# Rows of the fp16 value tiles 96 elements apart in place of 66

## The chip, the cores and the metric

The kernel runs on one core of a Trainium2 chip. Its engines have their own instruction streams: TensorE (PE in the profile, with PEld for its weight loads), VectorE (DVE), ScalarE (ACT), GpSimd (POOL) and SyncE (SP), which issues most of the transfers. The metric is the device time of one launch in microseconds. Before the change the median of three runs was 413.39 us (412.63 to 414.4).

## The reference

Cosine attention over 8 batches and 12 heads (448 positions, 64 features), then a mixer over tokens and channels. Everything arrives and leaves as float32.

```python
q_n = q / (norm(q) + 1e-6);  k_n = k / (norm(k) + 1e-6)
attn = softmax(q_n @ k_n.T / tau)                 # 448 x 448 per head, tau = 0.1
x = concat_heads(attn @ v)                        # (8, 448, 768)
h = relu(x.T @ w_tok1) @ w_tok2                   # 448 -> 256 -> 448 over tokens
u = x + h.T
out = u + relu(u @ w_ch1) @ w_ch2                 # 768 -> 1536 -> 768 over channels
```

## The kernel before

The unit of attention is a pair of heads of one batch: 8 batches x 6 pairs = 48 pairs. The 448 positions are cut into 4 chunks (NCH) of 112, one position of each chunk per partition. For pair i, `load` brings q, k and v to tiles ql, kl and vl, five pairs ahead. `squares`, `norm_sum`, `norm_root` and `norm_rec` make the inverse norms on GpSimd, VectorE and ScalarE; `normalize` writes the normed q and k in fp16 (tile qkn); `tpose_pe` (TensorE and a copy, in the first pairs) or `tpose_dma` (a transposing transfer) turns them (tile qkT). `score` (line 257) computes k times q per chunk of keys into PSUM tile pS, and `expo` (line 264) takes the exponential on ScalarE into tile pE in fp16.

The values take their own way. `v_cast` (line 214) casts vl, eight runs of 64 floats per partition (2 heads x 4 chunks), into one of four fp16 tiles v16s, used in turn by pair number. VectorE does 39 of these casts through `recast` (line 128) and ScalarE nine (line 220). A v16 tile has eight rows, one per head and chunk, each EV elements long: 64 values, a one in element 64, and the rest unused. The ones are written once, at the start (line 103), and give the sum of the exponentials as a 65th output column.

`pv` (line 267) then multiplies: for a block of 128 query positions and head h, four matmuls over the chunks c accumulate into one 65-column slice of PSUM tile pO. The 128 columns of pE are the stationary operand, and the 65 elements of row 4h + c of the value tile are the moving one. c = 0 starts the group (it overwrites) and c = 3 ends it:

```python
nc.tensor.matmul(pO[:, n, h, :], s["p"][:, c, h, c0:c0 + 128],
                 s["v16"][:, NCH * h + c, 0:E + 1],
                 start=(c == 0), stop=(c == NCH - 1))
```

Three blocks of positions are done in one call (24 matmuls), the fourth in another (8), so a pair has 32 and the kernel 1536. VectorE then takes the reciprocal of column 64 (line 284) and multiplies (line 285) into x16.

The mixer of a batch is a list of jobs: tokens up and down (`tok1` line 309, `tok2` line 322 and 327, in batch 0 their pairwise forms on lines 347 and 358), the residual add (line 331), a cast and a transposing transfer of u into uT (line 338), then channels up (`ch1`, line 375) and down (`ch2`, line 384), each with an evacuation by ScalarE (line 377) or VectorE (line 388), and the store.

The order on every engine is written out by hand. Pairs 0 to 12 run through `opening`, the others through `slot`, and `fill` puts mixer jobs between their steps by a credit of estimated matmul time. So mixer work of earlier batches fills TensorE between the attention steps of later ones, and after the last pair only mixer work remains.

The tiles of pool cst are laid out one after another: the identity, then the four value tiles, then all the rest, and the other pools behind them. The first value tile begins at byte 16768 of each partition, a multiple of 64.

Of the kernel before, what the change touches and what calls it, by code (L numbers as in the profile page):

```python
# [23 lines left out]
def kernel(  # L24
# [21 lines left out]
    B, H, S, E = q.shape  # L46
# [7 lines left out]
    NDH = D // DH  # L54
    NPAIR = H // 2
    NG = B // 2
    EV = E + 2
    inv_tau = 1.0 / float(tau)
    EPS_NORM = 1e-6

# [23 lines left out]
    id16 = cst.tile([128, 128], FP16, name="id16")  # L84
    v16s = [cst.tile([P, 2 * NCH, EV], FP16, name=f"v16_{n}") for n in range(4)]
    nns = [cst.tile([P, 2, 2 * NCH, 2], FP32, name=f"nn_{n}") for n in range(3)]
# [525 lines left out]
```

## Time and profile before

| what | value |
|---|---|
| median of three runs | 413.39 us |
| the profiled execution | 413.88 us |
| its span, first to last instruction | 411.5 us |
| PE busy | 383.9 us, 93% |
| ACT busy | 262.1 us, 64% |
| DVE busy | 233.9 us, 57% |
| POOL busy | 198.2 us, 48% |
| line 278, value matmuls | 1536, 64.8 us busy, 196 ns mean |
| line 128 on v, VectorE casts | 39, 24.9 us |
| granted TensorE clock, mean | 0.992 |

Busy time of one group is the union of its instructions. TensorE's matmuls overlap in the pipeline: one of line 278 is shown as 196 ns, but the next starts some 30 ns after it. The time that matters for such a row is therefore the distance between starts. The chain of waits is the work that ended last, followed back from the last instruction; a group's share of it is the time that the end depended on it in this execution.

### The profile page before, as it was taken

The page shows a single profiled execution, that of the slowest core. Times are in us where ns is not written, and L with a number is a line of the kernel's source. Part 1 is how long each engine was busy: PE and PEld are TensorE (multiplying, and loading weights), DVE is VectorE, ACT ScalarE, POOL GpSimd, SP SyncE. Part 2 cuts the span into 40 slices and gives each one's busy share as a digit, 9 for nine tenths or more (in the row PEclk, how much of TensorE's full clock was granted, in tenths as well). Part 3 has the DMA queues.
Part 4 walks back from the last instruction along what each step waited for, and adds up shares of the span by engine and source line. Part 5 has one row for each costly group of instructions (what it writes and reads, how often), then busy time and mean ns, then how long its engine had stood idle before and what let it go on. Part 6 is the DMA issues. An engine that isn't in the chain of part 4 may idle for free.

```text
span 411.5 us, 9002 instructions
## 1 busy us (share of the span) xinstructions
PE 383.9 (93%) x3592; PEld 220.6 (54%) x3592; DVE 233.9 (57%) x530; ACT 262.1 (64%) x452; POOL 198.2 (48%) x207
## 2 busy tenths in 40 slices
PE   2768789899999999999999999999999999999996
PEld 1456556556445556555545556555545556655453
DVE  4499978748634776548643676448643683152022
ACT  6879869876576666765677666775677665522400
POOL 4979969934743564634653464635563430000000
PEclk9989989999999999999999999999999999999999
DMA  8899999966974588649876488539963253027013
GB/s 212 239 247 216 221 252 234 248 139 140 238 155 109 139 181 198 160 75 184 219 178 150 124 196 198 151 84 199 209 166 91 61 120 101 2 43 149 0 43 112
DMA packets 97385, 63.63 MB, mean 155 GB/s; under 512 B 57536, under 2 KB 93888, under 8 KB 97344
## 3 DMA queue, kind: packets, MB, share of 16 engines
q1 hardware_dynamic: 94032, 58.20, 60.1%
q0 software_dynamic: 3184, 4.72, 6.7%
q8 instruction: 28, 0.46, 0.5%
q10 hardware_dynamic: 128, 0.15, 0.1%
q14 instruction: 13, 0.11, 0.1%
HBM read 43.45 MB, written 11.01 MB: 132 GB/s over the span
## 4 chain that ended last, share of the span: by engine, by line
PE 78%; DVE 11%; DMA 3%; ACT 3%; POOL 2%; issue 1%; DVEq 0%; POOLq 0%
PE pG L375 27%; PE pF L384 25%; PE pO L278 9%; PE pS L257 9%; PE pR L309 5%; PE pU L322 3%; DVE ssq L187 2%; DVE x L285 2%; ACT pE L264 2%; DMA uT<-u 1%; DVE qkT L246 1%; DMA kl<-in_k_dram 1%; POOL qkn L211 1%; DVE u L366 1%; DVE u L331 1%; POOL sq L177 1%
## 5 line engine op out<-in xcount | busy, mean ns | idle before, releaser
L264 ACT ACTIVATE pE<-pS 112x896 f16<-112x896 f32 x192 | 164.9, 914 | 39.5 <-PE pS L257 38.8
L375 PE MATMUL pG<-uT,wc1t 128*128 128x384 f16 (+1 forms) x576 | 121.4, 355 | 0.3 <-DMA uT<-u 0.3
L384 PE MATMUL pF<-wc2t,gT 128*128 128x384 f16 x672 | 116.6, 326 | 0.2
L211 POOL TENSOR_TENSOR qkn<-ql,rn 112x512 f16<-112x512 f32 x48 | 50.1, 1044 | 137.7 <-DVE rn L199 122.4
L384 PEld LDWEIGHTS <-gT 128*128 128x128 f16 x672 | 63.6, 98 | 47.0 <-issue 7.3
L377 ACT ACTIVATE gT<-pG 128x384 f16<-128x384 f32 (+1 forms) x96 | 52.6, 548 | 45.9 <-PE pG L375 45.1
L375 PEld LDWEIGHTS <-wc1t 128*128 128x128 f16 x576 | 51.7, 98 | 51.9 <-issue 11.5
L388 DVE TENSOR_TENSOR u<-pF,u 128x384 f32<-128x384 f32 x56 | 31.1, 556 | 78.5 <-PE pF L384 78.0
L257 PE MATMUL pS<-qkT 64*112 64x448 f16 x384 | 60.2, 384 | 13.2 <-DVE qkT L246 10.3
L278 PEld LDWEIGHTS <-pE 112*128 112x128 f16 x1536 | 60.8, 100 | 15.9 <-issue 5.4
L278 PE MATMUL pO<-v,pE 112*128 112x65 f16 x1536 | 64.8, 196 | 0.0
L187 DVE TENSOR_REDUCE ssq<-sq 112x16 f32<-112x1024 f32 (+1 forms) x49 | 58.3, 1192 | 5.5 <-ACT sq L175 3.7
L284 DVE RECIPROCAL rec<-pO 128x6 f32<-128x6 f32 x96 | 17.5, 182 | 77.1 <-PE pO L278 76.1
L211 POOL TENSOR_TENSOR qkn<-kl,rn 112x512 f16<-112x512 f32 (+1 forms) x48 | 49.8, 1038 | 0.0
L177 POOL TENSOR_TENSOR sq<-ql 112x512 f32<-112x512 f32 x46 | 48.8, 1061 | 1.6 <-ACT qkT L244 1.2
L177 POOL TENSOR_TENSOR sq<-kl 112x512 f32<-112x512 f32 x46 | 48.5, 1053 | 0.2 <-DMA kl<-in_k_dram 0.2
L285 DVE TENSOR_TENSOR x<-pO,rec 128x384 f16<-128x384 f32 x96 | 40.9, 426 | 3.3
L257 PEld LDWEIGHTS <-qkT 64*112 64x112 f16 x384 | 19.0, 127 | 39.1 <-issue 22.8
L128 DVE TENSOR_REDUCE v<-vl 112x512 f16<-112x512 f32 x39 | 24.9, 639 | 3.4 <-DMA vl<-in_v_dram 3.4
L331 DVE TENSOR_TENSOR u<-pU,x 128x384 f32<-128x384 f32 x50 | 25.4, 545 | 0.1
L337 ACT CAST u<-u 128x768 f16<-128x768 f32 x14 | 11.6, 832 | 20.9 <-DVE u L331 20.9
L191 ACT ACTIVATE ln<-ssq 112x16 f32<-112x16 f32 (+1 forms) x49 | 10.9, 223 | 17.7 <-DVE ssq L187 17.5
(41 smaller groups left out, 181.9 us busy)
## 6 DMA issues: line engine op xcount, KB each, us to landing
ql<-in_q_dram SPq DMA_DIRECT2D x48, 224.0 KB, 3.8
kl<-in_k_dram SPq DMA_DIRECT2D x48, 224.0 KB, 4.0
vl<-in_v_dram SPq DMA_DIRECT2D x48, 224.0 KB, 4.2
out_dram<-u SPq DMA_DIRECT2D x8, 336.0 KB, 3.5
wc1t<-in_moe_w_ch_dram POOLq DMA_DIRECT2D x4, 576.0 KB, 7.5
wc2t<-in_moe_w_ch_dram POOLq DMA_DIRECT2D x3, 768.0 KB, 10.3
out_dram<-u SPq DMA_DIRECT2D x8, 288.0 KB, 3.8
out_dram<-u SPq DMA_DIRECT2D x7, 240.0 KB, 3.1
```

The lines of the kernel that those rows point to most:

```text
L177: nc.gpsimd.tensor_mul(out=s["sq"][:, j], in0=a, in1=a)
L187: nc.vector.tensor_reduce(out=small(i, "ssq")[:, j], in_=st_[i]["sq"][:, j], axis=AXX.X, op=ALU.add)
L211: eng.tensor_tensor(out=o, in0=s[nm][:, g], in1=_bcast_free(rn, E), op=ALU.mult)
L257: nc.tensor.matmul(pS[:, h, 0:S], s["T"][64 * h:64 * h + 64, 1, c * P:(c + 1) * P], s["T"][64 * h:64 * h + 64, 0, :], start=True, stop=True)
L264: nc.scalar.activation(out=s["p"][:, c], in_=s["pS"][c][:, :, 0:S], func=AF.Exp, scale=inv_tau)
L278: nc.tensor.matmul(pO[:, n, h, :], s["p"][:, c, h, c0:c0 + 128], s["v16"][:, NCH * h + c, 0:E + 1], start=(c == 0), stop=(c == NCH - 1))
L285: nc.vector.tensor_tensor(out=xt[hp:hp + nr, t0:t0 + len(ts), d0:d0 + 2 * E].rearrange("p t (h e) -> p t h e", h=2), in0=pO[m0:128, :, :, ...
L331: nc.vector.tensor_tensor(out=u32[:, i - t0, cols], in0=pU[:], in1=xt[:, i, cols], op=ALU.add)
L375: nc.tensor.matmul(pG[:], wc1t[:, dt, ct * 128:(ct + 1) * 128], uT[:, dt, :], start=(dt == 0), stop=(dt == DT - 1))
L377: nc.scalar.activation(out=gT[:, ct, :], in_=pG[:], func=AF.Relu)
L384: nc.tensor.matmul(pF[:], gT[:, ct, (i - t0) * 128:(i - t0 + 1) * 128], wc2t[:, ct, dh * DH:(dh + 1) * DH], start=(ct == 0), stop=(ct == C ...
L388: nc.vector.tensor_tensor(out=o, in0=pF[:], in1=o, op=ALU.add)
```

## The change

Only the number of elements from one row of a value tile to the next changes. E is 64.

```diff
-    EV = E + 2
+    EV = 3 * E // 2
```

Rows were 66 fp16 elements, 132 bytes, apart, and a tile 1056 bytes. They are 96 elements, 192 bytes, apart, and a tile is 1536 bytes. In the tile at byte 16768, rows began at 0, 4, 8, 12, 16, 20, 24 and 28 bytes past a multiple of 64; now all begin at such a multiple. The second and fourth tile began 32 past a multiple of 64, and now begin at one. What is read and written of a row, 65 elements, stays the same, and so do all instructions and their order. Every tile allocated behind the value tiles moves up by 4 x 480 = 1920 bytes.

## The prediction

> **What bounds the kernel now.** I read the page of the slowest (only) core first, parts 1, 4 and 5, then the chain of waits in order of time, then the waits of TensorE, then the busy time by stretches, and last the value matmuls of line 278 one by one. Part 1 and part 4 of the page:
>
> ```profile
> PE 383.9 (93%) x3592; PEld 220.6 (54%) x3592; DVE 233.9 (57%) x530; ACT 262.1 (64%) x452; POOL 198.2 (48%) x207
> ...
> PE 78%; DVE 11%; DMA 3%; ACT 3%; POOL 2%; issue 1%; DVEq 0%; POOLq 0%
> PE pG L375 27%; PE pF L384 25%; PE pO L278 9%; PE pS L257 9%; PE pR L309 5%; PE pU L322 3%; DVE ssq L187 2%; DVE x L285 2%; ACT pE L264 2%; DMA uT<-u 1%; DVE qkT L246 1%; DMA kl<-in_k_dram 1%; POOL qkn L211 1%; DVE u L366 1%; DVE u L331 1%; POOL sq L177 1%
> ```
>
> TensorE sets the end for 78% of the span, and the one instruction whose input the change moves, line 278 (value rows streamed against exp columns), stands in the chain by itself. Ordering the chain by time gives its share with one more digit: 9.5%, or 0.095 x 411.5 = 39.1 us. That share is not spread evenly. The busy time of each engine by stretches shows three stages (columns: stretch, its length, busy time and instructions of PE, PEld, DVE, ACT, POOL, granted clock, DMA share, GB/s):
>
> ```profile
> 0.00:103.00 103.00, 81.39 (x967) 51.43 (x968) 75.21 (x172) 80.96 (x142) 75.69 (x88) 0.97 0.95 215
> 103.00:376.30 273.30, 271.33 (x2460) 152.93 (x2459) 153.63 (x350) 174.00 (x298) 122.52 (x120) 1.00 0.63 145
> 376.30:411.50 35.20, 31.18 (x169) 16.26 (x166) 5.02 (x9) 7.17 (x12) 0.00 (x0) 1.00 0.21 57
> ```
>
> From 103 to 376 us PE is busy 271.33 of 273.30 us and no other engine over 174; after 376 us there is no line 278 at all. Before 103 us PE shares the bound. The waits of PE from 57 us to the end confirm that it hardly waits:
>
> ```profile
> PE pS L257 <- DVE qkT L246: 1.7, 3, 1.0
> PE pU L322 <- DVE x L285: 1.2, 2, 0.6
> PE pG L375 <- DMA uT<-u: 0.3, 1, 0.3
> PE pS L257 <- ACT pE L264: 0.2, 1, 0.2
> ```
>
> Next, line 278 and the casts that write the value rows (what writes or reads tile v; ns min/median/max):
>
> ```profile
> L278 PE MATMUL pO<-v,pE x1536: 191/193/262, 15.5 to 358.0; 112*128 112x65 f16 x192
> L128 DVE TENSOR_REDUCE v<-vl x39: 627/628/686, 19.6 to 344.5; 112x512 f16<-112x512 f32 x39
> L220 ACT CAST v<-vl x9: 601/603/620, 11.3 to 282.9; 112x512 f16<-112x512 f32 x9
> L103 POOL MEMSET v<- x4: 133/135/137, 1.3 to 1.4; 112x8 f16 x4
> ```
>
> The 191 to 193 ns are a pipelined latency; what PE pays is the distance between starts. One block at full clock, in windows that all begin at 60.00 us and end just past one start, so that the bracket counts the matmuls begun by then:
>
> ```profile
> 60.00:60.17 0.17, 0.14 (x5) 1.00 1.07 265
> 60.00:60.20 0.20, 0.17 (x6) 1.00 1.05 257
> 60.00:60.30 0.30, 0.27 (x9) 1.00 1.04 266
> 60.00:60.33 0.33, 0.30 (x10) 1.00 1.07 276
> 60.00:60.42 0.42, 0.40 (x13) 1.00 1.07 282
> 60.00:60.45 0.45, 0.42 (x14) 1.00 1.04 278
> ```
>
> Matmuls 5, 9 and 13 each open a group of four (chunk c = 0); from one of them to the next matmul it is 0.03 us, and from there three matmuls take 0.10 and 0.09 us. Over every such start at full clock in the trace, the c = 0 matmul holds PE for 29.15 ns on average (29 or 30, never more; the first matmul after another line, 35.5 on average, is left out), and the c = 1, 2, 3 matmuls for 32.89, 32.49 and 32.50, together 32.64. This is the observation on which the forecast stands. The row of v read is 4h + c and starts 132 x (4h + c) bytes into the tile, so rows 0 and 4 start at a multiple of 16 bytes, and the other six 4, 8 or 12 bytes past one. Tiles 1 and 3 start 32 bytes off a multiple of 64, and row 4 lies 16 off; these read at 29 too. So a multiple of 64 is more than is needed; a multiple of 16 would do.
>
> **The change, part by part.** No instruction is added, removed or reordered, on any queue; the row pitch goes from 132 to 192 bytes.
>
> (1) *Value matmuls.* 24 of the 32 per pair start off a 16-byte boundary. If the boundary is the reason for the longer hold, each goes from 32.64 to 29.15, 3.49 ns less, 24 x 3.49 = 84 ns per pair, 48 x 84 = 4.0 us in all. By stage: 103 to 376 us holds 1056 of the 1536 matmuls, 33 pairs, 2.8 us, all on the path because PE has no slack there. From 57 to 103 us there are 230, 7.2 pairs, 0.6 us, of which I take two thirds, 0.4, since PE is not alone in the chain there. Before 57 us (8 pairs, 0.6 us) the chain runs through VectorE from pair to pair (qkT, u, ssq, rec, x follow each other without a gap), and two of those pairs run at granted clock 0.50, where the four chunks hold PE for 54, 54, 55 and 57 ns, so hardly anything is to be had: 0. Sum 3.2 us. The chain gives the same: 39.1 us of it on line 278, times 84 / 1017 (the 32 matmuls of a pair are 8 x 29.15 + 24 x 32.64 = 1017 ns), is 3.2. Bounds: 0 and 4.0.
>
> (2) *What is late next.* A block of 24 on the chain takes 0.77 us (24 x 32) and would take 0.70. Its reader, the reciprocal of line 284, waits for it already (76.1 us of idle ahead of it, 43 times), so it starts earlier with it. Nothing that PE waits on stands near in the long stretch: 1.2 us for x, 0.3 for the transposed u, and both are downstream of PE. At 102.41 us the chain passes through one 5.73 us transposing transfer, whose own ancestors are ssq, the residual add and a PE block at 96.63; a gain made before 98 us therefore goes through it.
>
> (3) *The casts.* They write eight runs of 64 elements, now at aligned starts. VectorE's 628 ns for 512 elements is below what its contiguous cast of the same kind makes of it (line 128 on w1s, 809 ns for 640, or 647 for 512), so there is no penalty to remove; bounds from that row are 0 to +19 ns each, 39 x 19 = 0.7 us of VectorE time, and v is not among the groups of the chain's shares. ScalarE's 603 lies between nothing and the same 19 ns, 9 times. The four memsets (135 ns) lie at 1.3 us, under the first loads. Taken as 0; the cover is VectorE's 120 us of idle in the long stretch.
>
> (4) *Everything behind v in memory moves up by 1920 bytes*, 15 x 128: the loads' tiles go from 128 past a multiple of 256 to a multiple of 256, and u, u32, uT and x from 64 to 192 past one. No row compares such places directly. The nearest: ql, kl and vl have the same shape and land in 3.8, 4.0 and 4.2 us, so 0.2 us either way for one transfer; the chain holds one load each of ql (2.78) and kl (5.38) and one transpose of u (5.73), hence -0.6 to +0.6. I take 0.
>
> Sum: 3.2 us, against the profiled execution's 413.88 (span 411.5 and 2.4 around it): 410.7. That execution is 0.49 above the median of the three runs, 413.39; from the median it is 410.2.
>
> [...]
>
> **The rivals.** (A) *The group's first matmul is short because it is first, not because of its row.* In this kernel c = 0 is both the aligned row and the one that overwrites instead of accumulating; the two can't be told apart by which rows are short. Against it: in the groups of 12 on line 384 the first and the later matmuls are alike (162 to 164 ns medians), in the pairs of line 358 too (55.5 and 55.0), and at half clock the three accumulating chunks differ among themselves (54, 55, 57) in the order of their byte offsets 4, 8, 12. For it: none of those other groups has a moving operand this short. If so, nothing changes: 413.4, with part (4) 412.8 to 414.0.
>
> (B) *The gain is real but eaten before the end,* by PE reaching a transfer or VectorE sooner. For it: 102.41, where PE's wait for uT is 0.3 us and any gain that does not go through the chain is lost. Against it: only 3.4 us of PE waits after 57 us. Losing everything before 103 us and a quarter of the rest leaves 2.1 us: 411.3.
>
> (C) *The other side: the transposing transfers of u become slower, since u16 and uT move from 64 to 192 past a multiple of 256.* Place: uT<-u, 31 issues of 3.7 us median, ahead of each batch's line 375. The one at 102.41 has no slack. It decides from the point where that 5.73 has grown by the 3.2 us gained elsewhere, 56%. If all double, it costs 5.7 us there, and the six later batches cost from nothing to 3.7 us each, as their slack allows; PE shows no wait for them now, so I take 0.3 each, 1.8: 410.2 + 5.7 + 1.8 = 417.7. Against it: the qkT transposes, from yet another start (128), land in 3.0 us and those of u, a seventh larger, in 3.7, which leaves little for the start to have done.
>
> **How the numbers follow.** Forecast (rows' start, 3.2 us, between 2.4 and 4.6 with part 4): 0.72, 408.8 to 411.0. (B) 0.08, 411.0 to 411.6. (A) 0.12, 412.8 to 414.0. (C) 0.08, 414 to 418. A measurement tells about 0.5%, 2.07 us, from no change: faster is at or below 411.32. The forecast lies below it nearly whole (0.72, less 0.02 for noise), (B) half: 0.74. Slower, above 415.46: most of (C), 0.07. The rest, 0.19, is the same. The range leaves out (C) and a little beyond each end: 408.6 to 414.0.
>
> **What would show it.** Right: line 278's medians go to 191 ns for all; blocks of 24 on the chain take 0.70 to 0.71 us in place of 0.77; the stretch that holds 1056 of them is 2.8 us shorter; lines 375 and 384 keep their means (355 and 326). If blocks stay at 0.77, (A) holds. If they shrink and the span doesn't, look at PE's waits for uT and x (B). If landings of uT exceed 3.7 us, (C). The prediction is wrong above all if c = 0 is short for being first.

## The result and the profile after

The changed kernel takes 410.84 us (median of 12 runs, 409.57 to 413.12) against 413.34 for the kernel before (12 runs, the three made first among them). The ratio is 0.9933, 95% interval 0.9913 to 0.9953; the two medians by themselves give 0.9940. The forecast was 410.2 in 408.6 to 414.0: right sign, and 2.5 us gained where 3.2 were forecast. The reason given for it turned out wrong, as the experiments show.

Parts 1 and 4 of the page after the change:

```profile
PE 380.6 (93%) x3592; PEld 217.7 (53%) x3592; DVE 233.7 (57%) x530; ACT 261.5 (64%) x452; POOL 197.9 (49%) x207
...
PE 80%; DVE 12%; DMA 3%; SPq 2%; ACT 1%; issue 1%; DVEq 0%
```

TensorE (PE) is still the bound, and busy 3.3 us less; the other engines' busy times are the same within 0.6. What writes and reads the value tiles (ns min/median/max):

```profile
L278 PE MATMUL pO<-v,pE x1536: 191/193/247, 15.6 to 353.7; 112*128 112x65 f16 x192
L128 DVE TENSOR_REDUCE v<-vl x39: 627/628/687, 19.0 to 340.2; 112x512 f16<-112x512 f32 x39
L220 ACT CAST v<-vl x9: 601/603/621, 11.7 to 279.1; 112x512 f16<-112x512 f32 x9
```

The casts did not change (627/628/687 ns against 627/628/686), and neither did the 191/193 ns that a value matmul is shown with, of which 191 for all had been expected. The change is in the spacing, which shows in the blocks of 24 on the chain in order of time (start us, length us). After, and then before:

```profile
104.27 0.73 PE pO L278 x24
111.67 0.73 PE pO L278 x24
120.36 0.73 PE pO L278 x24
127.77 0.73 PE pO L278 x24
```

```profile
114.50 0.76 PE pO L278 x24
123.24 0.77 PE pO L278 x24
130.70 0.77 PE pO L278 x24
```

0.73 instead of the forecast 0.70. One by one at full clock, from the start of a matmul to the next start, the four chunks c = 0 to 3 now hold PE for 30.17, 30.64, 30.11 and 30.14 ns (before 29.15, 32.89, 32.49, 32.50). The slow three became faster and c = 0 became slower. The starts show how: about four matmuls follow at 29 or 30 ns and then one at 35, over and over, whichever chunk it is.

Where the time went is read by taking the start of the same matmul, by its number (counted from 0), in both traces. Both issue their 3592 matmuls in the same order.

| matmul | before, us | after, us | ahead by |
|---|---|---|---|
| 100th | 24.99 | 24.37 | 0.62 |
| 400th | 47.71 | 47.10 | 0.61 |
| 500th | 58.37 | 56.16 | 2.21 |
| 1000th | 106.92 | 104.47 | 2.45 |
| 3300th | 357.49 | 353.17 | 4.32 |

The first 0.62 us are no effect of the rows: the 100th matmul starts anywhere from 23.35 to 24.99 us in the kernels of this document, and the earliest of them has the slow rows. Between the 1000th and the 3300th lies the long stretch bound by PE, before and then after (the columns are those of the stretches in the prediction):

```profile
106.92:357.49 250.57, 248.60 (x2306) 139.50 (x2303) 143.89 (x329) 167.62 (x288) 118.60 (x117) 1.00 0.64 149
```

```profile
104.47:353.17 248.70, 246.92 (x2306) 137.88 (x2303) 143.90 (x329) 167.29 (x288) 118.50 (x117) 1.00 0.62 150
```

It is 1.87 us shorter, and by line (start to next start) 1.66 of it is line 278, 35.07 to 33.41. Another 0.33 is line 257, 33.42 to 33.09, which takes anything from 33.05 to 33.71 in kernels with either spacing and is scatter. The 1.6 us between the 400th and the 500th matmul are not the rows' doing: in this execution before, PE's granted clock was 0.50 in 53.3 to 56.7 us, and in this execution after it was 1.00 there, while it was half from 52 or 53 us on in three of the experiments whose rows are as fast (e1, e2, e5). So the two profiled spans differ by 4.3 us and the medians by 2.5.

What PE waits for after 57 us is, after the change (before: 1.7, 1.2 and 0.2, and 0.3 for uT):

```profile
PE pS L257 <- DVE qkT L246: 1.8, 3, 1.1
PE pU L322 <- DVE x L285: 1.3, 2, 0.7
PE pS L257 <- ACT pE L264: 0.2, 1, 0.2
```

### The profile page after: what moved, and what is told of

It is laid out like the page before. It is cut to its first block, busy times and chain, and to the rows that moved or that the text cites. A ratio compares the mean times of both kernels' runs of the same rounds, so it can differ in the third digit from the quotient of the medians.

```text
span 407.2 us, 9002 instructions
## 1 busy us (share of the span) xinstructions
PE 380.6 (93%) x3592; PEld 217.7 (53%) x3592; DVE 233.7 (57%) x530; ACT 261.5 (64%) x452; POOL 197.9 (49%) x207
## 4 chain that ended last, share of the span: by engine, by line
PE 80%; DVE 12%; DMA 3%; SPq 2%; ACT 1%; issue 1%; DVEq 0%
PE pG L375 27%; PE pF L384 26%; PE pO L278 9%; PE pS L257 9%; PE pR L309 5%; PE pU L322 3%; DVE ssq L187 2%; DVE x L285 2%; DMA ql<-in_q_dram 2%; DVE qkT L246 2%; DVE u L366 1%; DMA vl<-in_v_dram 1%; SPq L164 1%; DVE u L331 1%; DVE v L128 1%
## 5 line engine op out<-in xcount | busy, mean ns | idle before, releaser
L388 DVE TENSOR_TENSOR u<-pF,u 128x384 f32<-128x384 f32 x56 | 31.1, 555 | 77.9 <-PE pF L384 77.6
L278 PEld LDWEIGHTS <-pE 112*128 112x128 f16 x1536 | 58.2, 99 | 15.7 <-issue 5.1
L278 PE MATMUL pO<-v,pE 112*128 112x65 f16 x1536 | 62.1, 195 | 0.0
```

The costliest lines, as they stand in the source:

```text
L388: nc.vector.tensor_tensor(out=o, in0=pF[:], in1=o, op=ALU.add)
```

## The experiments

The theory first held was the prediction's: a row is read slowly if it does not start at a multiple of 16 bytes. Rivals were its rival (A), that the first matmul of a group is short, and that the place of the other tiles brought the gain.

**e1: a multiple of 16 bytes, not of 64.**

```diff
-    EV = E + 2
+    EV = E + 8
```

> Rows 72 elements (144 bytes) apart, so that each starts at a multiple of 16 bytes but mostly not of 64. If a start at a multiple of 16 bytes is what counts: line 278 keeps the spacing of the changed kernel (29 ns, every fifth 35; 30.3 on average), blocks of 24 take 0.73 us, and the time is that of the changed kernel, 410.8 (ratio to before 0.993). If 64 bytes are needed: rows at 16, 32 and 48 past a multiple hold PE for 32.6 ns again, and the time is 413.3 (ratio 1.000).

410.95 us, ratio 0.9940 [0.9912, 0.9968]; chunks 30.15, 30.73, 30.07, 30.14, blocks of 24 in 0.73 us. A multiple of 64 is not needed.

**e2: rows 96 apart, but all starting 4 bytes past a multiple of 64.** The rest lies where the changed kernel has it. The lines are set against the kernel before, as in all experiments but e9.

```diff
-    EV = E + 2
+    EV, VO = 3 * E // 2, 2
...
-            nc.gpsimd.memset(t[:, :, E:E + 1], 1.0)
+            nc.gpsimd.memset(t[:, :, VO + E:VO + E + 1], 1.0)
...
-        o = s["v16"][:, :, 0:E]
+        o = s["v16"][:, :, VO:VO + E]
...
-                                     s["v16"][:, NCH * h + c, 0:E + 1],
+                                     s["v16"][:, NCH * h + c, VO:VO + E + 1],
```

> Rows 96 apart as in the changed kernel, all tiles at the same addresses, but the 65 elements of each row moved up by two, so that every row, that of c = 0 too, starts 4 bytes past a multiple of 64. If the row's start is the cause: all four chunks hold PE for 32.5 to 33 ns, c = 0 no longer 29; 32 x (32.8 - 30.3) = 80 ns per pair above the changed kernel, 3.8 us in all, some 3.1 on the path: 413.9 (ratio 1.001, a little above before, whose c = 0 rows were aligned). If c = 0 is short because it opens the group: c = 0 stays at 29 and the time is 413.3. If the move of the tiles behind brought the gain: 410.8.

410.98 us, ratio 0.9934 [0.9910, 0.9958]; chunks 29.54, 31.15, 29.74, 29.19, 29.9 on average. Blocks on its chain:

```profile
105.54 0.72 PE pO L278 x24
112.93 0.72 PE pO L278 x24
121.61 0.72 PE pO L278 x24
```

Rows that all start 4 bytes past a 16-byte boundary are as fast as aligned ones. The theory on which the forecast stood falls here.

**e3: only the other tiles moved,** by an unused tile behind the value tiles; rows 66 apart.

```diff
-    nns = [cst.tile([P, 2, 2 * NCH, 2], FP32, name=f"nn_{n}") for n in range(3)]
+    pad = cst.tile([P, 960], FP16, name="pad"); nns = [cst.tile([P, 2, 2 * NCH, 2], FP32, name=f"nn_{n}") for n in range(3)]
```

> Rows 66 apart as before, and an unused tile of 1920 bytes behind the four value tiles, so that everything else lies where the changed kernel has it. If the gain is all the rows': 413.3, spacing 29 / 32.9 / 32.5 / 32.5 as before (ratio 1.000). If the new place of the load tiles brings part of it: 412.7 (0.9985) and an earlier start of the first value matmuls by up to 0.6 us; all of it: 410.8 (0.993).

413.43 us, ratio 0.9983 [0.9962, 1.0003]; chunks 29.15, 32.93, 32.49, 32.48, and the long stretch 250.20. Two of its blocks on the chain:

```profile
105.03 0.76 PE pO L278 x24
112.48 0.77 PE pO L278 x24
```

The place of the other tiles does nothing to the spacing. Its half-clock matmuls are worth a look: 57, 54, 54 and 55 ns for the four chunks, over and over, where the prediction had read 54, 54, 55 and 57 in the order of the byte offsets. The rows are the same, so that order does not belong to the offsets. Four of them take 220 ns in the kernel before, in e3 and in e1, whose rows are fast at full clock: in these traces the slow rows cost nothing at half clock.

**e4: streams of matmuls alone,** 96 of each form with a new stationary each, rows 128 elements apart; nothing else is computed. One line of it, wrapped here, 65 columns 4 bytes past a multiple of 64 (`mv(n, off, cols)` takes row n % 8 of a fp16 tile from byte `off` on, `st(n)` one of twelve stationary operands):

```python
for n in range(96): nc.tensor.matmul(ps[n // 4 % 3][0:128, 65 * (n // 12 % 2):65 * (n // 12 % 2) + 65],
                                     st(n), mv(n, 4, 65), start=(n % 4 == 0), stop=(n % 4 == 3))
```

> Leaves out the whole computation: it runs streams of 96 matmuls on TensorE, one form per line, and stores zeros and a few sums. 65 columns, groups of four, a new stationary for each. Row start theory: 0, 16 and 32 bytes past a multiple of 64 give 30.3 ns per matmul (2.9 us for 96), 2 to 14 bytes give 32.6 to 33 (3.1 us), with or without accumulation. Group opening theory: the start makes no difference, and the stream in which every matmul opens its own group is short at 12 bytes past too (2.8 us). [...]

Each window below runs from the first start of a stream to the first start of the next, so its length (second column) over 96 is the spacing. The other columns are PE's busy time, the matmuls in flight in the window, the clock, DMA share and GB/s. In order: 65 columns at 0, 4 and 12 bytes, 65 at 12 bytes with every matmul opening its own group; then, at 0 bytes, 57, 62, 64, 66 and 80 columns.

```profile
23.34:26.25 2.92, 2.92 (x97) 1.00 0.02 6
29.20:32.08 2.88, 2.88 (x102) 1.00 0.00 0
40.80:43.70 2.90, 2.90 (x102) 1.00 0.00 0
52.48:55.38 2.90, 2.90 (x102) 1.00 0.00 0
66.01:68.57 2.56, 2.56 (x103) 1.00 0.03 6
68.57:71.28 2.72, 2.72 (x103) 1.00 0.02 6
71.28:74.08 2.80, 2.80 (x102) 1.00 0.00 0
74.08:77.00 2.92, 2.92 (x102) 1.00 0.02 6
86.26:89.70 3.44, 3.44 (x101) 1.00 0.00 0
```

The start (30.0 to 30.8 ns over ten offsets) and the group's opening (2.90 us for 96 at 12 bytes either way) hardly count. At this pitch no stream of 65 columns averages the 31.8 of before, so neither theory explains it, and what is left is the pitch of 66 itself. The widths bear on the 35 ns of every fifth matmul. The averages are 26.67 ns for 57 columns, 28.33 for 62, 29.16 for 64, 30.30 for 65, 30.31 for 66, 31.67 for 70, 33.64 for 73 and 35.83 for 80. From 64 to 80 that is 0.417 ns a column, (35.83 - 29.16) / 16. With this slope the averages of 62, 64, 70 and 80 all lie 2.5 ns above columns times 0.417. Those of 65, 66 and 73 do not: they lie near 72, 72 and 80 times 0.417 (30.0, 30.0, 33.4), and that of 57 at 64 times (26.7), the width rounded up to a multiple of 8. The larger of the two, an estimate read off these eight averages, fits them within 0.35 ns. No stream here has 65 columns at 29.15 on average, the least being 30.0. Four matmuls at 29 ns and one at 35 average 30.2, so the 35 ns go with that average; what makes them is not shown. The weight loads alone do not set that average: 33 and 49 columns came out at 25.0 ns with the same weight loads.

**e5: only the order of the chunks.** The new theory came from the layout: at 132 bytes, row 1 begins at byte 132, in the 16 bytes (128 to 143) in which row 0, bytes 0 to 129, has just ended. So do rows 2 and 3 behind 1 and 2, and 5, 6 and 7. Row 4 begins at 528 and row 3 ends at 525, on the two sides of a boundary. c = 0 is thus not only aligned and first, it is also the one chunk whose row does not begin where the last one ended. The experiment keeps pitch and memory of before:

```diff
-                for c in range(NCH):
+                for c in (1, 3, 0, 2):
...
-                                     start=(c == 0), stop=(c == NCH - 1))
+                                     start=(c == 1), stop=(c == 2))
```

> Rows 66 apart as before and nothing moved in memory; only the order in which the four chunks of a group are multiplied is 1, 3, 0, 2 in place of 0, 1, 2, 3, so that no matmul streams the row that lies right behind the row streamed just before. New theory (a row is slow if it begins in the 16 bytes in which the row just streamed ended, as rows 1, 2, 3, 5, 6, 7 do at 132 bytes and rows 0 and 4 don't): no chunk at 32.5 ns any more, 30.0 to 30.5 on average, and the gain of the changed kernel without its pitch, 410.9 (ratio 0.993 to 0.994). Rival (a change of the start's offset from one row to the next, or the odd pitch itself, costs): offsets still change with every row, spacing stays near 31.8 on average, time as before (ratio 1.000). Rival (the group's first matmul is short): the first, now chunk 1, takes 29, the others 32.6, time as before.

411.29 us, ratio 0.9933 [0.9904, 0.9961], the changed kernel's within the interval. In the order of issue the matmuls hold PE for 29.22, 30.45, 29.16 and 31.39 ns, 30.06 on average, and its chain has

```profile
122.94 0.72 PE pO L278 x24
130.34 0.73 PE pO L278 x24
```

Nothing was aligned and nothing moved. What brought the average from 31.77 to 30.06 ns is which row follows which. (The order of the stationary operands changed with it; in e6 it stays and the rows alone change their order.)

**e6: streams at other pitches and orders,** with rows `pitch` elements apart.

> Leaves out the whole computation: streams of 96 matmuls with a new stationary each, one form per line. Theory of the shared 16 bytes: rows in order at pitch 66 give 29 / 32.9 / 32.5 / 32.5 (31.8 on average, 3.05 us for 96) and the same if each matmul opens its own group; rows in the orders 0 2 4 6 1 3 5 7 and 1 3 0 2 5 7 4 6 give 30.0 to 30.8 (2.9 us), also row 0 or row 1 always; pitches 72, 74, 76, 80, 82, 96, 98 and 130 give 30.0 to 30.8, pitches 65, 68 and 70 lie between, as some of their rows begin in the line in which the one before ended. 64 columns at pitch 64 and 66: 29.2 both, no row shares. 73 columns at pitch 74 longer than at 80 (33.6) by 1.5 or more. Theory that a changing offset costs: the two other orders and the pitches 74, 76, 82 and 98 are as slow as pitch 66 in order, about 31.8. Theory that the group's opening is short: every stream shows 29 for its first of four, and the stream in which each matmul opens a group is all 29.

In the order of the windows: pitch 66 in order; the same with every matmul opening its own group; rows 0 2 4 6 1 3 5 7; rows 1 3 0 2 5 7 4 6; rows backwards; pitch 65; pitch 68; pitch 96; then 64 columns at pitch 64 and at pitch 66; last, 73 columns at pitch 74 and at pitch 80.

```profile
24.73:27.77 3.04, 3.04 (x97) 1.00 0.03 5
27.77:30.82 3.04, 3.04 (x102) 1.00 0.02 5
30.82:33.71 2.89, 2.89 (x102) 1.00 0.00 0
33.71:36.60 2.89, 2.89 (x102) 1.00 0.02 6
36.60:39.50 2.90, 2.90 (x102) 1.00 0.02 6
48.28:51.38 3.10, 3.10 (x102) 1.00 0.02 5
51.38:54.36 2.98, 2.98 (x101) 1.00 0.03 6
71.80:74.71 2.91, 2.91 (x102) 1.00 0.02 6
80.47:83.27 2.80, 2.80 (x102) 1.00 0.02 6
83.27:86.18 2.91, 2.91 (x102) 1.00 0.03 6
...
89.06:92.45 3.39, 3.39 (x102) 1.00 0.00 0
92.45:95.69 3.24, 3.24 (x101) 1.00 0.03 5
```

Pitch 66 in order is slow (31.7 ns) whoever opens the group, which ends rival (A); in the three orders in which no row shares it is fast (30.1 to 30.3 ns). Rows 0 and 1 in turn, where every second matmul shares, average 31.1. Pitch 65, where seven of eight rows share, is the slowest of the 65 columns (32.3). At pitch 68 the rows alternate, 29.2 for the even and 32.4 to 33.5 for the odd: row 2 begins at 272 and row 1 ends at 265, in the same 32 bytes but not the same 16. Backwards, where a row ends near the place where the one before began, is one of these three, 2.90 us for 96. The 64 columns at pitch 66 had been expected fast; they average 30.3, with rows 2, 3, 6 and 7 at 31.4 to 33.1. Counting again, row 1 ends at 259 and row 2 begins at 264, both in 256 to 271, and rows 3, 6 and 7 share likewise, rows 1 and 5 don't: the expectation had been miscounted, and the theory holds row by row there. 73 columns at pitch 74 cost 35.3 against 33.8, and 129 columns at pitch 130 58.3 against 56.7 at pitch 136.

Two expectations failed. Pitch 65 was to lie between the fast streams and pitch 66 in order, and lies above both, as more of its rows share. Pitch 70, where rows 1 and 5 share, was to lie between too, and tells what a slow row costs: it averages 30.4, no more than streams without sharing. Its rows 1 and 5 hold PE for 34.4 ns, the other six for 29.1. At pitch 76, where none shares, two of the eight hold it for 33 ns and six for 29, 30.0 on average. So in these streams one row's 33 ns are no sign of sharing; the average is. A quarter of sharing rows hardly shows (30.4 at pitch 70, 30.3 at pitch 96 with none), half of them make it 31.0 (pitch 68), three quarters 31.7 (pitch 66), seven eighths 32.3 (pitch 65).

**e12: half of it in the kernel,** rows 68 apart.

```diff
-    EV = E + 2
+    EV = E + 4
```

> Rows 68 elements (136 bytes) apart: rows 1, 3, 5 and 7 begin in the 16 bytes in which the row before ended, rows 2, 4 and 6 don't. Theory of the shared 16 bytes: spacing 29, 32 to 33, 29, 32 to 33 for chunks 0 to 3, 31.0 on average, about half of the gain on the value matmuls: the stretch from the 1000th to the 3300th matmul falls by 0.9 us, ratio near 0.997. If only starts at a multiple of 16 bytes are fast (the rule of the prediction): rows 1, 2, 3, 5, 6, 7 slow, ratio 1.000 but for rows 2 and 6, which start 8 bytes past one, slow as before.

Chunks 29.18, 32.79, 29.14 and 32.67 ns, blocks of 24 in 0.74 and 0.75 us, the long stretch 249.38, ratio 0.9961 [0.9941, 0.9981]. Row 2, 8 bytes past a boundary, went from 32.49 to 29.14. Its tiles behind the values moved by 128 bytes, which puts the loads at a multiple of 256, so the ratio holds that effect too, whatever it is worth.

**e7, e8, e9, e10, e11: the place of the other tiles.** e7 and e11 are e3 with 1024 in place of 960 elements, a move by 2048, which leaves everything as far from a multiple of 256 as before. e8 is e5 with the pad of e3, e10 is e3 again beside e11, and e9 puts 64 unused bytes ahead of the mixer's tiles in the changed kernel (`gap64 = mix.tile([P, 32], FP16, name="gap64")`).

> Rows 66 apart as before, everything behind the value tiles moved by 2048 bytes in place of 1920, so that the places relative to a multiple of 256 are those of before (loads, qkn and qkT 128 past one). If the move by 1920 helped because loads and transposing transfers then begin at a multiple of 256: the qkT transposes land in 3.0 us as before (2.7 in the changed kernel and with the move by 1920), and the time is that of before, ratio 1.000. If any move helps, or that was scatter: 2.7 us or a ratio near 0.998.

> Rows 66 apart, the order of chunks 1, 3, 0, 2, and everything behind the value tiles moved by 1920 bytes: both effects of the change, without its pitch. If they add up: qkT transposes 2.7 us, value matmuls 30.2 ns on average, the stretch from the 1000th to the 3300th matmul 248.7 us as in the changed kernel (249.14 with the order alone, 250.20 with the move alone, 250.57 before), ratio 0.992 to 0.994. If the move gives nothing: 249.1 and a ratio like that of the order alone, 0.9933.

> The changed kernel with 64 unused bytes ahead of the mixer's tiles, so that x16, u32, u16, uT and gT too begin at a multiple of 256 (192 past one in the changed kernel). If a start at a multiple of 256 helps the transposing transfers of u as it seems to help those of qkn: uT lands in 3.4 us or less (3.9 in the changed kernel), and the time is the changed kernel's or up to 0.5 us better, since PE hardly waits for uT: ratio 0.992 to 0.9933. If not: 3.7 to 4.0 us, ratio 0.9933.

> The move by 1920 bytes alone once more, beside the move by 2048 on the same chip, since 0.9983 and 1.0019 came from different calls. If a start at a multiple of 256 is worth something to the whole: this one is 0.7 us or more ahead of the move by 2048. If the difference was scatter: both within 0.2% of before and of each other.

> The move by 2048 bytes beside the move by 1920: see there. qkT transposes again 3.0 to 3.1 us here and 2.7 there in either case.

| kernel | qkT lands in, us | ratio, 95% interval |
|---|---|---|
| e3, moved 1920 | 2.7 | 0.9983 [0.9962, 1.0003] |
| e10, the same again | 2.7 | 0.9968 [0.9949, 0.9986] |
| e7, moved 2048 | 3.1 | 1.0019 [1.0000, 1.0039] |
| e11, the same again | 3.0 | 0.9990 [0.9976, 1.0003] |
| e5, order alone | 3.1 | 0.9933 [0.9904, 0.9961] |
| e8, order and moved 1920 | 2.7 | 0.9934 [0.9911, 0.9958] |
| e9, changed kernel, mixer at 256 too | 2.7 | 0.9944 [0.9922, 0.9967] |

The transposing transfers of qkn, by the transfers' landing times of e3 and e7:

```profile
qkT<-qkn SPq DMA_TRANSPOSE x34, 2.7
```

```profile
qkT<-qkn SPq DMA_TRANSPOSE x34, 3.1
```

They land 0.3 to 0.4 us sooner wherever the tiles start at a multiple of 256, in all twelve kernels. Those of u land in 3.9 us both in the changed kernel, from 192 past such a multiple, and in e9, from one. What this is worth to the whole is not settled. With the slow rows, the move by 1920 is ahead of the move by 2048 by 0.36% and 0.22%, 1.5 and 0.9 us, with intervals that overlap; with the fast order it adds nothing (0.9933 and 0.9934). No stretch of the traces shows where such a gain would lie. Line 278 by itself accounts for 2.0 of the change's 2.5 us, which leaves some 0.5 us for this and everything else.

No run beat the changed kernel beyond its interval.

## Why the prediction was right, and where not

- *That PE is the bound, and that line 278 passes its gain on:* right. The long stretch shortened by 1.87 us, 1.66 of it line 278's own.
- *Step (1), the cause ("if the boundary is the reason"):* wrong. Rows 4 bytes past a boundary are fast (e2), and unaligned rows at the old pitch are fast in another order (e5, e6). In these runs the rows that begin in the 16 bytes in which the row streamed just before ended are the slow ones (32.49 to 32.89 ns before, 32.67 and 32.79 in e12, where the others take 29.14 to 29.18); 96 elements apart none does. The trace held a hint that was not used: the adjacency of the rows divides them as the alignment does, with c = 0 the odd one in both, and as the opening of a group does. One observation was taken as evidence for one of three causes that it could not tell apart. The support from half clock was none: the order 54, 55, 57 does not go with the rows (e3).
- *Step (1), the size:* 84 ns per pair forecast, 48 measured: 32 x (31.77 - 30.27). It was assumed that all rows would reach the 29.15 of c = 0. In these traces a 65-column matmul holds that only beside slower ones; the streams of 65 columns in e4 average 30.0 to 30.8, and c = 0 rose from 29.15 to 30.17. (The first matmul after another line, left out there, averages 35.1 in the blocks of 24 and not 35.5; nothing rests on it.) For 33 pairs 48 ns make 1.6 us, as measured, where 2.8 were forecast; from 57 to 103 us it was 0.33 where 0.4 was forecast.
- *Step (2), nothing late next:* right. PE's wait for uT (0.3) is gone, and no wait of PE after 57 us grew by more than 0.1. The 5.73 us transfer at 102.41 us is on the chain no more: from 86 to 110 us the chain now runs through TensorE alone.
- *Step (3), the casts at 0:* right, 627/628/687 against 627/628/686.
- *Step (4), the moved tiles at 0:* open. Two comparisons with slow rows allow 0.9 and 1.5 us, beyond its bound of 0.6, with intervals that overlap, and the one with fast rows none. The landing times of qkT, which the prediction did not price, did change.
- *Rival (A):* ruled out by e5 and e6. *Rival (B):* not seen. *Rival (C):* uT lands in 3.9 us where it took 3.7, but kernels with either place gave 3.6 to 4.0, and PE does not wait for it. Its text has an error: the transfers of u (128 x 768) are a seventh smaller than those of qkn (112 x 1024), not larger.

That the sum came near is luck in two ways: a wrong cause made the same forecast of which rows would gain, and a gain put too high (3.2) met some 0.5 us that line 278 does not account for. Where those come from is not shown. One candidate beside the moved tiles is the granted clock, which averaged 0.9925 in the 57 runs of kernels with fast rows (the changed one, e1, e2, e5, e8, e9) and 0.9909 in the 85 runs of the kernel before beside the experiments; by how the time falls with the clock within each group, that is an estimated 0.15 to 0.3 us.

## What to carry to other kernels

Here fp16 matmuls of 65 columns, streaming rows that lie behind one another, started 31.77 ns apart with rows that meet in the same 16 bytes, 30.27 with an unused gap so wide that they don't, and 30.06 with the rows in another order, which costs no memory. In a kernel with such matmuls, see where one row ends and the next begins, and try either. Before a spacing in a trace is put down to one property of an operand, list what else sets the short instances apart, and find a form that separates them; here a change of order alone would have told. And don't take the fastest instance of a group (29.15 ns here) as what all can reach (30.27).

## What was not expected of the hardware

- The 65-column fp16 rows that begin in the 16 bytes in which the last one ended held PE for 32 to 34.5 ns at full clock (before, e6, e12); the streams without such rows averaged 30.0 to 30.8 (e4, e6). In e6 such rows held it for 36 to 37 ns against 33.8 at 73 columns, for 39 against 37.0 at 81 and for 59 against 56.7 at 129. In its streams of 65 columns, two such rows in eight cost 0.1 ns per matmul, six in eight 1.4.
- In e4, 65 and 66 columns both averaged 30.3 ns and 64 columns 29.16. The 65th column, which holds the ones in the kernel, cost 1.1 ns there, not the 0.42 that a column costs on average from 64 to 80.
- In e4, a stationary of 112 columns in place of 128 made the stream slower, 51.7 ns per matmul against 30.3, and 64 columns did not make it faster (31.7).
- Over the twelve kernels, the transposing transfers of qkn landed in 2.7 us from a start at a multiple of 256 and in 3.0 to 3.1 from 128 past one; those of u in 3.6 to 4.0 from any of the three starts tried (64 and 192 past one, and at one).
